# Slot table from one-hots of 64, logits on four column groups, and half of the first low weight halves back on VectorE

## The chip, the cores and the metric

The kernel runs on one core of a Trainium2 chip. The time is that of one execution on the device in microseconds (us); a kernel is run several times, and the median counts.

## The reference: windowed attention, then a two-level mixture of experts

```python
# q, k, v: (8, 8, 576, 64) f32
scores = q @ k.transpose(0, 1, 3, 2) / 8
# heads 0 to 3: 0 <= i - j < 32; heads 4 to 7: 0 <= i - j < 128 and (i - j) % 4 == 0
scores = np.where(masks[None], scores, -1e9)
attn = softmax(scores) @ v
x = attn.transpose(0, 2, 1, 3).reshape(4608, 512)
# 4 groups of 4 experts, one group and one expert in it per token
g_idx = argmax(x @ w_group); g_w = softmax(x @ w_group)[g_idx]
e_idx = argmax(x @ w_expert[g_idx]); e_w = softmax(x @ w_expert[g_idx])[e_idx]
h = maximum(x @ w1[g_idx, e_idx], 0)        # 512 -> 1024
out = g_w * e_w * (h @ w2[g_idx, e_idx])    # 1024 -> 512
```

Each of the 4608 tokens goes to one of 16 experts. A matmul of f32 quality is made from two f16 halves of each operand, high and low, and three products of them.

## The kernel before: 36 attention steps with the routing woven in, then 16 experts

**Attention.** The batches go in pairs (`bp`, 0 to 3), and each pair in nine steps of 64 positions, so there are 36 steps `s` and three more to empty the pipeline. In step `s` TensorE (PE) computes `scores(s)`, `av(s - 2)` (probabilities times values), `transpose_p(s - 1)` and `transpose_x(s - 3)`; VectorE (DVE) takes the maxima `mx` (L281) and differences `d` (L283) of the scores, and with `den` (L362, L364) normalises the result to `x` (L369); ScalarE (ACT) does the exponentials and copies. `o`, the PSUM tile of `av`, exists once, so that `av` of one step waits for `x` of the step before. GpSimd (POOL) makes shifted copies of `v` (`shift_v`, L130 to L137, tile `vs`, two in turn, one for three steps), and for the first group of a pair clears the part of `kb` that carries keys over (L118).

**Routing.** After the nine steps of a pair, `turned_logits` (L416, then L417 on ACT) computes the gate logits of its 1152 tokens, nine tiles of 128 (`TPB`), and the generator `route` does the rest in pieces. `slot()` is called between DVE's attention instructions and runs pieces as long as a credit lasts, which grows by `RATE[bp]` a call. A piece that yields 2 closes a gate: what follows, PE work, is put behind the next step's `av`. `route` transposes the logits (L424, `lg_ps`), finds group and expert (L433 to L456, the one-hot `E`), counts ranks by matmuls (L462 to L467, `rk_ps`), and turns each token's slot, an expert's base plus a rank, into a table of tokens by slot: a one-hot `ohl` of the slot's low 7 bits (L506) times `mv`, a one-hot of its high part times the token's number (L495, L502), summed over tiles by matmuls (L517, `tb_ps`), added into `tab` (L538 to L543). `own` is a PSUM tile that holds small operands of DVE.

**Hand-over.** For the two experts that have most tokens after two and three pairs, weights are loaded early (`prefetch`, `load_weights`): eight chunks of 128x1024, the high half `h` on ACT (L640), the low half `l` on DVE (L637), or with `aside`, for the first expert, on GpSimd (L634, L635). Their first 128 and 256 tokens are computed beside the last steps and the last routing; there the order is the string `TAIL`, a letter for a piece: `r` of the last routing, `a` and `b` of the first and second expert, `w` a chunk of weights, `T` the end of the routing's PSUM tiles. After it the experts follow one another (L726 first layer, L734 low half `hl` of its result, L819 and L837 second layer).

PE and DVE have their orders from the code (`manual_schedule`, L926), SP and ACT as well from the start (L140); GpSimd's is left to the scheduler until the experts.

## Time and profile before

| what | value |
|---|---|
| median of 3 runs | 571.64 us (571.36 to 571.8) |
| profiled execution, own time | 573.72 us |
| its span | 572.0 us |
| mean granted TensorE clock | 0.995 of full speed |
| busy share: PE, PEld, DVE, ACT, POOL | 94%, 68%, 66%, 56%, 38% |
| DMA | 134.32 MB, mean 235 GB/s |

PEld is the loading of weights into TensorE, which overlaps its matmuls. A share is an average over the attention steps (to some 150 us), the hand-over and the experts, which have different limits; idle time of an engine costs something only where another waits for it.

### The profile page before, as it was taken

How to read it: one execution, taken by the hardware profiler on the slowest of the kernel's cores; microseconds unless marked ns; L12 is line 12 of the kernel's file. 1: busy time of each engine (PE TensorE's matmuls, PEld its weight loads, DVE VectorE, ACT ScalarE, POOL GpSimd, SP SyncE). 2: the span in 40 equal slices, each digit the busy share in tenths (PEclk: the TensorE clock that was granted, in tenths of full speed). 3: DMA queues.
4: the chain of work that ended last, by engine and by line, in shares of the span. 5: the costliest groups of instructions: out<-in, count | busy, mean ns of one | idle time of the engine just before them, and what ended most of it. 6: DMA issues, size and time to landing. Idle time of an engine off the chain costs nothing. (4 is left out here: it accounts for less than half of the span.)

```text
span 572.0 us, 16623 instructions
## 1 busy us (share of the span) xinstructions
PE 539.1 (94%) x6652; PEld 390.1 (68%) x6652; DVE 376.4 (66%) x853; ACT 318.7 (56%) x563; POOL 218.2 (38%) x204
## 2 busy tenths in 40 slices
PE   4999999997797999999999999999999999999975
PEld 2788778786675676557666667576675775797873
DVE  8675886968778337464859597755757757766730
ACT  6464554565654236464656465565666665774631
POOL 6795554649920423402140523225153231121202
PEclk9999999999999999999999999999999999999989
DMA  7988878799672716968697786969879899879811
GB/s 275 390 282 262 311 271 269 257 312 283 187 254 62 235 41 173 296 156 243 191 280 199 250 216 210 295 187 311 211 241 293 239 285 321 223 275 296 221 60 30
DMA packets 79266, 134.32 MB, mean 235 GB/s; under 512 B 42988, under 2 KB 52630, under 8 KB 79186
## 3 DMA queue, kind: packets, MB, share of 16 engines
q1 hardware_dynamic: 72258, 113.65, 65.7%
q0 software_dynamic: 6784, 19.51, 10.4%
q8 instruction: 54, 0.88, 0.6%
q14 instruction: 26, 0.21, 0.1%
q10 hardware_dynamic: 144, 0.07, 0.1%
HBM read 106.16 MB, written 19.29 MB: 219 GB/s over the span
## 5 line engine op out<-in xcount | busy, mean ns | idle before, releaser
L790 POOL DMA_INDIRECT out<-yr,sent x31 | 35.3, 1139 | 218.9 <-ACT yr L789 205.9
L734 DVE SCALAR_TENSOR_TENSOR hl<-a,hh 128x256 f16<-128x256 f32 (+13 forms) x144 | 60.8, 423 | 83.2 <-ACT hh L733 83.1
L726 PE MATMUL a<-xs,wb1h 128*128 128x256 f16 (+7 forms) x576 | 97.7, 275 | 2.1 <-DVE hl L734 2.1
L726 PE MATMUL a<-xs,wa 128*128 128x304 f16 (+7 forms) x864 | 98.3, 275 | 0.3 <-SPq L1134 0.3
L733 ACT ACTIVATE hh<-a 128x256 f16<-128x256 f32 (+13 forms) x144 | 55.9, 388 | 65.8 <-PE a L726 64.3
L726 PEld LDWEIGHTS <-wa 128*128 128x128 f16 x864 | 80.7, 99 | 17.0 <-SPq L1134 0.5
L637 DVE SCALAR_TENSOR_TENSOR wa<-w,wa 128x1024 f16<-128x1024 f32 x56 | 67.7, 1217 | 27.6 <-ACT wa L640 27.6
L819 PEld LDWEIGHTS <-hh 128*128 128x128 f16 x480 | 46.9, 98 | 54.8 <-issue 1.2
L640 ACT ACTIVATE wa<-w 128x1024 f16<-128x1024 f32 x64 | 67.2, 1055 | 21.0 <-DMA w<-wpack 16.3
L726 PE MATMUL a<-xs,wb1l 128*128 128x256 f16 (+7 forms) x288 | 78.3, 275 | 0.0
L819 PE MATMUL y<-wa,hh 128*128 128x512 f16 x240 | 73.9, 379 | 0.0
L726 PEld LDWEIGHTS <-wb1h 128*128 128x128 f16 x576 | 55.0, 98 | 14.5 <-issue 2.6
L665 POOL DMA_INDIRECT xr<-xd,sent x41 | 41.6, 1014 | 38.0 <-DVE key L590 14.5
L637 DVE SCALAR_TENSOR_TENSOR wb2l<-w,wb2h 128x1024 f16<-128x1024 f32 x32 | 38.6, 1220 | 20.3 <-ACT wb2h L640 20.3
L313 PE MATMUL o<-vs,pt 128*32 128x130 f32 x576 | 40.6, 274 | 8.8 <-DVE x L369 3.7
L302 ACT COPY pt<-t 128x512 f32<-128x512 f32 x36 | 21.1, 586 | 49.1 <-PE t L301 48.5
L789 ACT ACTIVATE yr<-y,cs 128x512 f32<-128x512 f32 (+3 forms) x31 | 21.3, 686 | 44.2 <-PE y L819 32.3
L819 PE MATMUL y<-wb2h,hh 128*128 128x512 f16 x120 | 45.6, 380 | 0.0
L819 PE MATMUL y<-wa,hl 128*128 128x512 f16 x120 | 45.5, 379 | 0.0
L819 PE MATMUL y<-wb2h,hl 128*128 128x512 f16 x120 | 45.5, 379 | 0.0
L819 PE MATMUL y<-wb2l,hh 128*128 128x512 f16 x120 | 45.5, 379 | 0.0
L640 ACT ACTIVATE wb2h<-w 128x1024 f16<-128x1024 f32 x32 | 33.2, 1052 | 16.3 <-DMA w<-wpack 16.0
(202 smaller groups left out, 1069.2 us busy)
## 6 DMA issues: line engine op xcount, KB each, us to landing
w<-wpack SPq DMA_DIRECT2D x128, 512.0 KB
kb<-k SPq DMA_DIRECT2D x24, 384.0 KB
vt<-v SPq DMA_DIRECT2D x14, 390.0 KB
qb<-q SPq DMA_DIRECT2D x7, 768.0 KB
xd<-x SPq DMA_DIRECT2D x24, 192.0 KB
wa<-v SPq DMA_DIRECT2D x6, 390.0 KB
wa<-q SPq DMA_DIRECT2D x3, 768.0 KB
xd<-x SPq DMA_DIRECT2D x32, 48.0 KB
```

The lines of the kernel that those rows point to most:

```text
L302: nc.scalar.copy(pt[n % NPT], t)
L313: nc.tensor.matmul(o[32 * j : 32 * j + 32, c // 2, at : at + 130], pt[n % NPT][:, c, 32 * j : 32 * j + 32], t[:, :, jl, bb * 4 + c, :], st ...
L637: nc.vector.scalar_tensor_tensor(l, w32, SW, h, ALU.mult, ALU.subtract)
L640: nc.scalar.mul(parts(i)[0], w32s[i], SW)
L665: nc.gpsimd.indirect_dma_start(out=xr[0:n], out_offset=None, in_=xd[0:known, :], in_offset=bass.IndirectOffsetOnAxis(ap=ent[0:n, t : t + 1 ...
L726: nc.tensor.matmul(a[:, 0:cap], ww[:, c * FF + f * P : c * FF + f * P + P], xx[:, c, 0:cap], start=(i == 0), stop=(i == len(mm) - 1),)
L733: nc.scalar.activation(hh[:, f, 0:cap], a[:, 0:cap], AF.Relu)
L734: nc.vector.scalar_tensor_tensor(hl[:, f, 0:cap], a[:, 0:cap], 0.0, hh[:, f, 0:cap], ALU.max, ALU.subtract)
L789: nc.scalar.activation(yr[0:n, :], yp[0:n, :], AF.Copy, scale=cs[0:n, t : t + 1])
L790: ins = nc.gpsimd.indirect_dma_start(out=out, out_offset=bass.IndirectOffsetOnAxis(ap=ent[0:n, t : t + 1], axis=0), in_=yr[0:n, :], in_off ...
L819: nc.tensor.matmul(yp, h[:, f, t * P : t * P + n], ww[:, f * DM : f * DM + DM], start=(i == 0), stop=(i == len(mm) - 1),)
```

## The change: smaller one-hots, GpSimd's products, a fourth column group

A slot's low part now has 6 bits, so `ohl` has 64 columns, in one DVE instruction. An expert has 8192 slots of room (`REG`), so that the bits above say only which of the first eight blocks of 64 a token is in: DVE makes `okm`, a one-hot of eight per token. GpSimd multiplies it by the token's number and then by the expert's one-hot `E`, once for the even and once for the odd blocks, into `mv`. The table's matmuls write 64 partitions each, two for each tile. The logits run on four column groups of PE (32 columns each) instead of three: four tiles at a time, and for the ninth each group adds one quarter of the features, summed when `id4` turns them. Of the first expert's eight low halves, four (the second, fourth, sixth and eighth) go to DVE. GpSimd's order is taken from the code, too; `RATE` and `TAIL` have new values.

```diff
-RATE = (0.23, 0.3, 0.45)
+RATE = (0.2, 0.25, 0.4)
-TAIL = "ararrrarrawrawwrawbwarrrrrrrbrrwbrrwbrrrrwbrrrrTwbbb"
+TAIL = "ararrrarrawrrawrwarrrwbwarrrbrwrbrrwbrrrwbrrrTwbbb"
-REG = NTOK + P
+REG = 8192
...
+    id4 = cp.tile([P, 32], F32, name="id4")
+    nc.vector.tensor_reduce(id4, id32.rearrange("p (q m) -> p m q", q=4), axis=AX.X, op=ALU.add)
...
-        lt_ps = psR.tile([96, 3, P], F32, name="lt_ps", tag="r")
+        lt_ps = psR.tile([P, 3, P], F32, name="lt_ps", tag="r")
         for i in range(3):
             chains = []
-            for j in range(3):
-                a0 = (3 * i + j) * P
+            for j in range(4):
+                a0 = min(4 * i + j, TPB - 1) * P
                 cuts = [a0] + [S] * (a0 < S < a0 + P) + [a0 + P]
-                chains.append([(c, j, a, b, a0) for a, b in zip(cuts, cuts[1:]) for c in range(4)])
+                own_c = range(4) if i < 2 else (j,)
+                chains.append([(c, j, a, b, a0) for a, b in zip(cuts, cuts[1:]) for c in own_c])
...
-                    nc.tensor.matmul(ov, wg[:, c], mv, start=(c == 0), stop=(c == 3))
+                    nc.tensor.matmul(ov, wg[:, c], mv, start=(c == 0 or i == 2), stop=(c == 3 or i == 2))
...
-        for i in range(3):
-            nc.tensor.transpose(
-                lg_ps[:, 3 * i : 3 * i + 3].rearrange("p t n -> p (t n)"), lt[:, i], id32[0:96, 0:96]
-            )
+        for i in range(2):
+            nc.tensor.transpose(lg_ps[:, 4 * i : 4 * i + 4].rearrange("p t n -> p (t n)"), lt[:, i], id32)
+        nc.tensor.matmul(lg_ps[:, TPB - 1], lt[:, 2], id4, start=True, stop=True)
...
-        mv = T("mv", [TPB, NE * NK4], F16)
+        okm = T("okm", [TPB, 2 * NK4])
         nc.vector.tensor_tensor(
-            mv,
-            high_v.unsqueeze(1).broadcast_to([P, TPB, NE * NK4]),
-            hl[:, 1].unsqueeze(2).broadcast_to([P, TPB, NE * NK4]),
+            okm,
+            low_v[:, 0 : 2 * NK4].unsqueeze(1).broadcast_to([P, TPB, 2 * NK4]),
+            hl[:, 1].unsqueeze(2).broadcast_to([P, TPB, 2 * NK4]),
             ALU.is_equal,
         )
-        yield 0.75
-        nc.vector.tensor_tensor(mv, mv, mine_v.unsqueeze(2).broadcast_to([P, TPB, NE * NK4]), ALU.mult)
-        yield 0.75
-        ohl = T("ohl", [TPB, P], F16)
-        for t0 in range(0, TPB, 3):
-            nc.vector.tensor_tensor(
-                ohl[:, t0 : t0 + 3],
-                low_v.unsqueeze(1).broadcast_to([P, 3, P]),
-                hl[:, 0, t0 : t0 + 3].unsqueeze(2).broadcast_to([P, 3, P]),
-                ALU.is_equal,
+        mv = T("mv", [2, TPB, NE, NK4], F16)
+        nc.gpsimd.tensor_tensor(okm, okm, mine1.unsqueeze(2).broadcast_to([P, TPB, 2 * NK4]), ALU.mult)
+        okv = okm.rearrange("p t (k h) -> p h t k", h=2)
+        for h in range(2):
+            nc.gpsimd.tensor_tensor(
+                mv[:, h],
+                Ef[:, 0:TPB].unsqueeze(3).broadcast_to([P, TPB, NE, NK4]),
+                okv[:, h].unsqueeze(2).broadcast_to([P, TPB, NE, NK4]),
+                ALU.mult,
             )
-            if t0 < TPB - 3:
-                yield 0.55
+        yield 0.2
+        ohl = T("ohl", [TPB, 64], F16)
+        nc.vector.tensor_tensor(
+            ohl,
+            low_v.unsqueeze(1).broadcast_to([P, TPB, 64]),
+            hl[:, 0].unsqueeze(2).broadcast_to([P, TPB, 64]),
+            ALU.is_equal,
+        )
+        yield 2
         yield 2
...
         for t in range(TPB):
-            nc.tensor.matmul(tb_ps, ohl[:, t], mv[:, t], start=(t == 0), stop=(t == TPB - 1))
+            for h in range(2):
+                nc.tensor.matmul(
+                    tb_ps[64 * h : 64 * h + 64],
+                    ohl[:, t],
+                    mv[:, h, t].rearrange("p e k -> p (e k)"),
+                    start=(t == 0),
+                    stop=(t == TPB - 1),
+                )
...
-            todo.extend(load_weights(ev[r], wsets[r], r == 0))
+            todo.extend(load_weights(ev[r], wsets[r], lambda i: r == 0 and i % 2 == 0))
...
-    man.enter_context(tc.manual_schedule(engines={ET.PE, ET.DVE}))
+    man.enter_context(tc.manual_schedule(engines={ET.PE, ET.DVE, ET.Pool}))
```

The order in which instructions stand shows what this moves; the lines of the changed kernel are numbered differently there. First GpSimd near the start: the shifts of `v` into the two tiles `vs`, and the memset of `kb` (L118). Before:

```order
L130 TENSOR_SCALAR vs_112<-vt_110 64x2x1040
L133 TENSOR_SCALAR vs_112<-vt_110 64x2x520
L137 TENSOR_SCALAR vs_113<-vt_110 64x2x520
L118 MEMSET kb_115 128x2x256
L130 TENSOR_SCALAR vs_113<-vt_111 64x2x1040
L133 TENSOR_SCALAR vs_113<-vt_111 64x2x520
L130 TENSOR_SCALAR vs_113<-vt_111 64x2x520
```

And now, where the same memset stands:

```order
L130 TENSOR_SCALAR vs_112<-wa_92 64x2x520
L133 TENSOR_SCALAR vs_112<-wa_92 64x2x520
L130 TENSOR_SCALAR vs_113<-vt_110 64x2x1040
L135 MEMSET vs_113 64x2x520
L133 TENSOR_SCALAR vs_113<-vt_110 64x2x520
L118 MEMSET kb_115 128x2x256
L130 TENSOR_SCALAR vs_113<-vt_110 64x2x520
```

The memset stood ahead of the second tile's first shift (from `vt_111`); now it stands behind the shifts of two more groups (from `vt_111` and from `wa_92`) and most of the fourth's (`vt_110` again).

Second DVE, where the third pair's routing begins (`pm`, `oh`, `E` are pieces of the argmax, `mx` and `d` of attention). Before:

```order
L448 TENSOR_REDUCE pm_2529<-own 128x45
L369 TENSOR_TENSOR x<-o,den 128x512
L451 TENSOR_TENSOR oh_2536<-own,pm_2529 128x180
L456 TENSOR_TENSOR E_206<-oh_2536 128x144
L281 TENSOR_REDUCE mx<-s 128x8
L283 TENSOR_TENSOR d<-s,mx 128x4x2x64
L362 TENSOR_SCALAR den<-o 128x8
L477 TENSOR_TENSOR rks<-rk_ps,E_206 128x144
```

And now (L642 is the low half of a weight chunk, L637 before):

```order
L440 TENSOR_REDUCE pm_2547<-own 128x45
L361 TENSOR_TENSOR x<-o,den 128x512
L443 TENSOR_TENSOR oh_2554<-own,pm_2547 128x180
L642 SCALAR_TENSOR_TENSOR wa_91<-w_2190,wa_91 128x1024
L273 TENSOR_REDUCE mx<-s 128x8
L448 TENSOR_TENSOR E_208<-oh_2554 128x144
L275 TENSOR_TENSOR d<-s,mx 128x4x2x64
L354 TENSOR_SCALAR den<-o 128x8
L356 RECIPROCAL den<-den 128x8
```

A low half stands ahead of `E`, and the ranks' first instruction (L477 before, L469 now) comes a whole step later.

Third DVE in the hand-over, where the last pair is routed beside the second expert's weights (`wb1l` is one of its low halves). Before:

```order
L451 TENSOR_TENSOR oh_3176<-own,pm_3158 128x180
L734 SCALAR_TENSOR_TENSOR hl<-a,hh 128x128
L637 SCALAR_TENSOR_TENSOR wb1l<-w_3016,wb1h 128x1024
L637 SCALAR_TENSOR_TENSOR wb1l<-w_3018,wb1h 128x1024
L456 TENSOR_TENSOR E_207<-oh_3176 128x144
L637 SCALAR_TENSOR_TENSOR wb1l<-w_3020,wb1h 128x1024
```

And now:

```order
L443 TENSOR_TENSOR oh_3200<-own,pm_3182 128x180
L448 TENSOR_TENSOR E_209<-oh_3200 128x144
L739 SCALAR_TENSOR_TENSOR hl<-a,hh 128x128
L642 SCALAR_TENSOR_TENSOR wb1l<-w_3034,wb1h 128x1024
L642 SCALAR_TENSOR_TENSOR wb1l<-w_3036,wb1h 128x1024
L469 TENSOR_TENSOR rks<-rk_ps,E_209 128x144
L471 COPY base_159<-rk_ps 128x16
```

`E` moved ahead of the two low halves. On PE the ranks, which need it, moved from behind the first expert's second layer to ahead of it.

## Rows read from the trace of the kernel before

**Rows 1.** The page's busy tenths of PE in 40 equal slices of the span.

```profile
PE   4999999997797999999999999999999999999975
```

**Rows 2.** Busy time by stretches of 20 us: the stretch, its length, then for each engine the busy us and the number of instructions, the granted clock as a share of full speed, the DMA share and GB/s. Engines in order: PE, PEld, DVE, ACT, POOL.

```profile
160.00:180.00 20.00, 17.45 (x167) 13.24 (x165) 17.96 (x41) 12.51 (x21) 1.16 (x2) 1.00 0.58 196
...
220.00:240.00 20.00, 20.00 (x148) 11.72 (x147) 13.73 (x24) 12.05 (x19) 4.41 (x5) 1.00 0.99 280
```

**Rows 3.** The timeline of PE: start, length of the row, line, operation, tiles. L254 begins a step, L271 are its scores, L313 its `av`, L462 the ranks, L517 the table. In brackets the idle time before, and what ended it.

```profile
38.21 1.08 PE L271 MATMUL s<-kb,qb 128*32 128x128 f32 x32
...
57.74 0.38 PE L254 MATMUL s<-masks,idb 128*128 128x512 bf16 x1
...
64.86 0.44 PE L462 MATMUL rk_ps<-base,id 128*128 128x160 f32 x2
...
65.56 0.38 PE L254 MATMUL s<-masks,idb 128*128 128x512 bf16 x1
...
79.78 0.42 PE L517 MATMUL tb_ps<-mv,ohl 128*128 128x64 f16 x9
80.04 0.38 PE L254 MATMUL s<-masks,idb 128*128 128x512 bf16 x1
...
83.18 0.38 PE L254 MATMUL s<-masks,idb 128*128 128x512 bf16 x1
...
92.76 0.38 PE L254 MATMUL s<-masks,idb 128*128 128x512 bf16 x1
...
118.36 0.38 PE L254 MATMUL s<-masks,idb 128*128 128x512 bf16 x1
...
128.53 0.38 PE L254 MATMUL s<-masks,idb 128*128 128x512 bf16 x1
...
136.15 0.27 PE L313 MATMUL o<-vs,pt 128*32 128x130 f32 x1 [1.04 <-DVE top L564]
...
140.53 0.27 PE L313 MATMUL o<-vs,pt 128*32 128x130 f32 x1 [1.04 <-DVE x L369]
...
146.60 0.42 PE L517 MATMUL tb_ps<-mv,ohl 128*128 128x64 f16 x9
```

**Rows 4.** The timeline of POOL, same columns: shifts of `v` (L130, L133, L137), memsets of `kb` (L118) and `vs` (L135).

```profile
17.48 1.05 POOL L137 TENSOR_SCALAR vs<-vt 64x1040 f32<-64x1040 f32 x1
19.74 0.53 POOL L118 MEMSET kb<- 128x512 f32 x1 [1.21 <-PE s L271]
22.35 1.93 POOL L130 TENSOR_SCALAR vs<-vt 64x2080 f32<-64x2080 f32 x1 [2.08 <-DMA vt<-v]
24.36 1.05 POOL L133 TENSOR_SCALAR vs<-vt 64x1040 f32<-64x1040 f32 x1
...
28.65 0.96 POOL L135 MEMSET vs<- 64x1040 f32 x1
...
35.10 1.93 POOL L130 TENSOR_SCALAR vs<-vt 64x2080 f32<-64x2080 f32 x1
```

**Rows 5.** The timeline of PE: the first pair's logits (80 records, two for each f32 matmul), and the transposes of the logits.

```profile
49.41 2.93 PE L416 MATMUL lt_ps<-xT,wg 128*32 128x128 f32 x80
...
57.49 0.41 PE L424 MATMUL lg_ps<-id,lt 96*128 96x96 f32 x3
```

**Rows 6.** Groups of DVE instructions of one shape between 50 and 190 us: line, operation, tiles, out and in (partitions x elements, type), count, then busy us in total, mean ns of one, idle us before them.

```profile
L506 DVE TENSOR_TENSOR ohl<-own,hl 128x384 f16<-128x384 f32 x12 | 6.4, 536 | 0.0
L637 DVE SCALAR_TENSOR_TENSOR wb2l<-w,wb2h 128x1024 f16<-128x1024 f32 x4 | 4.9, 1214 | 0.0
...
L495 DVE TENSOR_TENSOR mv<-own,hl 128x576 f16<-128x576 f32 x4 | 3.0, 753 | 0.0
L502 DVE TENSOR_TENSOR mv<-mv,own 128x576 f16<-128x576 f16 x4 | 3.0, 743 | 0.0
...
L538 DVE TENSOR_SCALAR own<-tb_ps 128x64 f32<-128x64 f32 x4 | 0.9, 218 | 0.0
```

**Rows 7.** The timelines of POOL (two low-half pieces of the first expert) and of DVE beside them, and one more L646 of DVE with POOL idle.

```profile
148.97 2.14 POOL L635 TENSOR_TENSOR wa<-w,wa 128x1024 f16<-128x1024 f32 x1
151.08 1.05 POOL L634 TENSOR_SCALAR w<-w 128x1024 f32<-128x1024 f32 x1
...
149.64 1.52 DVE L646 TENSOR_TENSOR sel<-tab,top 128x32 f32<-128x32 f32 x1
...
151.41 0.74 DVE L653 CAST ente<-twoe 128x2 int32<-128x2 f32 x1
...
182.93 0.23 DVE L646 TENSOR_TENSOR sel<-tab,top 128x48 f32<-128x48 f32 x1
```

**Rows 8.** The timelines of PE and DVE in the hand-over.

```profile
163.19 0.38 PE L819 MATMUL y<-wa,hh 128*128 128x512 f16 x1
...
175.95 0.26 PE L517 MATMUL tb_ps<-mv,ohl 128*128 128x64 f16 x3 [1.50 <-DVE ohl L506]
...
180.50 0.38 PE L726 MATMUL a<-xs,wb1h 128*128 128x256 f16 x2 [1.16 <-DVE hl L734]
...
182.73 0.38 PE L726 MATMUL a<-xs,wb1h 128*128 128x256 f16 x2 [0.76 <-DVE hl L734]
...
163.22 0.33 DVE L451 TENSOR_TENSOR oh<-own,pm 128x180 f32<-128x180 f32 x1
...
166.44 0.30 DVE L456 TENSOR_TENSOR E<-oh 128x144 bf16<-128x144 f32 x1
```

More of the change, by code (lines that the diff above doesn't have):

```diff
@@ L173, in moe_attention_kernel @@
     own = psV.tile([P, 512], F32, name="own")
-    low_v, high_v, pri, mine_v = own[:, 0:P], own[:, P : P + NE * NK4], own[:, 192:196], own[:, 196 : 196 + TPB]
+    low_v, pri = own[:, 0:64], own[:, 192:196]
     oh_v = own[:, 208 : 208 + 20 * TPB].rearrange("p (n e) -> p n e", e=4)
@@ L209, in moe_attention_kernel @@
     slots = cp.tile([P, NCHK], F32, name="slots")
-    high = cp.tile([P, NE, NK4], F32, name="high")
-    nc.gpsimd.iota(
-        high,
-        pattern=[[REG // P, NE], [1, NK4]],
-        base=0,
-        channel_multiplier=0,
-        allow_small_or_imprecise_dtypes=True,
-    )
-    nc.vector.tensor_copy(low_v, low)
-    nc.vector.tensor_copy(high_v, high.rearrange("p e k -> p (e k)"))
-    nc.vector.tensor_copy(mine_v, mine1)
+    nc.vector.tensor_copy(low_v, low[:, 0:64])
     tab = cp.tile([P, NE, NK4], F32, name="tab")
@@ L403, in turned_logits @@
     def turned_logits(bp):
-        lt = sm.tile([96, 3, P], F32, name="lt")
-        lt_ps = psR.tile([96, 3, P], F32, name="lt_ps", tag="r")
+        lt = sm.tile([P, 3, P], F32, name="lt")
+        lt_ps = psR.tile([P, 3, P], F32, name="lt_ps", tag="r")
         for i in range(3):
             chains = []
-            for j in range(3):
-                a0 = (3 * i + j) * P
+            for j in range(4):
+                a0 = min(4 * i + j, TPB - 1) * P
                 cuts = [a0] + [S] * (a0 < S < a0 + P) + [a0 + P]
-                chains.append([(c, j, a, b, a0) for a, b in zip(cuts, cuts[1:]) for c in range(4)])
+                own_c = range(4) if i < 2 else (j,)
+                chains.append([(c, j, a, b, a0) for a, b in zip(cuts, cuts[1:]) for c in own_c])
             for k in range(max(map(len, chains))):
@@ L422, in route @@
         lg_ps = psR.tile([P, TPB, 32], F32, name="lg_ps", tag="r")
-        for i in range(3):
-            nc.tensor.transpose(
-                lg_ps[:, 3 * i : 3 * i + 3].rearrange("p t n -> p (t n)"), lt[:, i], id32[0:96, 0:96]
-            )
+        for i in range(2):
+            nc.tensor.transpose(lg_ps[:, 4 * i : 4 * i + 4].rearrange("p t n -> p (t n)"), lt[:, i], id32)
+        nc.tensor.matmul(lg_ps[:, TPB - 1], lt[:, 2], id4, start=True, stop=True)
         T = lambda nm, shape, dt=F32: sm.tile([P] + shape, dt, name=nm)
@@ L487, in route @@
         nc.vector.tensor_copy(sl_v[:, 2], slots[:, mine])
-        nc.vector.tensor_single_scalar(sl_v[:, 1], sl_v[:, 2], 7, ALU.arith_shift_right)
+        nc.vector.tensor_scalar(sl_v[:, 1], sl_v[:, 2], 6, P - 1, ALU.arith_shift_right, ALU.bitwise_and)
         yield 0.35
-        nc.vector.tensor_single_scalar(sl_v[:, 0], sl_v[:, 2], P - 1, ALU.bitwise_and)
+        nc.vector.tensor_single_scalar(sl_v[:, 0], sl_v[:, 2], 63, ALU.bitwise_and)
         hl = T("hl", [2, TPB], F16)
@@ L608, in order, with load_weights @@
         nc.vector.tensor_copy(ordi[:, NEARLY:NE], ordf[:, NEARLY:NE])
-    def load_weights(ev, w, aside=False):
+    def load_weights(ev, w, aside=lambda i: False):
         src = wpack[bass.ds(ev * P, P), :]
@@ L632, in chunk @@
                 h, l = parts(i - 1)
-                if aside:
+                if aside(i - 1):
                     nc.gpsimd.tensor_scalar(w32, w32, SW, 1.0, ALU.mult, ALU.mult)
```

## The prediction

> **What bounds the kernel now.** I read the page first: its row of TensorE (PE) slices shows nines almost everywhere and sevens near a quarter of the span [rows 1]. The busy time by stretches then says where PE can gain: 17.45 of 20 us are busy at 160 to 180, 20.00 at 220 to 240, with the granted clock at full speed in both [rows 2]. Whatever delays PE after its expert matmuls have become continuous costs its own length, and before that only PE's own work, and waits of PE, can move the end. So I followed PE by its timeline through the attention steps and the hand-over to the experts (up to about 186 us), and looked at the other engines where PE waits.
>
> One attention step without routing takes 3.14 us of PE: from 80.04 to 83.18 [rows 3]. Seven such steps are 21.98. The seven from 57.74 to 83.18, in which the first batch pair is routed, take 25.44; PE's own routing matmuls in them are 0.70 for the ranks (64.86 to 65.56) and 0.26 for the table (79.78 to 80.04), so PE waits 2.5 us. The second pair's seven, from 92.76 to 118.36, hold 25.60 - 21.98 - 0.96 = 2.66 us of waits; the third pair's four, from 128.53 to 146.60, 18.07 - 12.56 - 0.70 = 4.8 [rows 3]. The waits of the third end about when VectorE (DVE) has written `x`, or another of its pieces, with 1.04 us each at 136.15 and 140.53: DVE is full there, and its work counts one to one.
>
> The profiled execution took 573.72 us around a span of 572.0. The runs' median is 571.64, 2.08 lower, so I sum the changes of the profiled span and add the sum to 571.64. Three runs lie within 0.44 us; I call anything within 0.2% (1.14 us) no change.
>
> **The change part by part.**
>
> *GpSimd in program order: +1.6.* Before, GpSimd ran the memset of the carried keys (L118, `kb`) at 19.74, while it had nothing better to do: it then waited until 22.35 for `v` to land [rows 4]. Now the memset stands behind the third group's shifts. In the row before, the third group's large shift starts at 35.10, with GpSimd busy without a break since 22.35. Now it has as many pieces ahead of it (L137 twice and no L135, instead of once each, 1.05 against 0.96 us), so it starts at 35.2. It takes 1.93, the memset L135 0.96, one shift of 1.05, and then L118 0.53; with three gaps of 0.08 (22.35 + 1.93 to 24.36) that ends at 39.9 [rows 4]. PE wants those keys at 38.21 [rows 3], so it waits about 1.6 us, in steps that hold no other wait to absorb it. Bounds: 0, if the queue ahead shortens, and 1.9. The later two memsets come in stretches in which GpSimd is not behind, and I cost them at nothing; its slack covers them.
>
> *Logits on four column groups: -2.2.* Today 40 matmuls per pair take 2.93 us [rows 5]. Three chains run side by side, of 128 columns a round: four rounds for the first three tiles, five for the second three (the tile cut at 576 has eight halves on one group, and its last four run nearly alone), four for the third: 13 rounds of 128 columns, 0.225 us a round. With four chains it is 4, then 5.5 (the same eight halves), then one for the ninth tile: 10.5 rounds, 2.37 us. Four pairs give -2.2. If a fourth chain gains nothing, 0; if time falls as 3 to 4, -0.73 a pair. The Trainium skill (TensorEngine Tiling (Array Packing), Performance Considerations) promises up to four times for weights of 32 columns. By it alone the step from three groups to four would be 3/4, -2.9 in all. I keep -2.2, because the ordered rounds already account for the 2.93 of the row.
>
> *Turning the logits back, and the table: +0.7.* Three passes of 96 columns take 0.25 us (57.49 to 57.74) [rows 3, 5]. Two passes of 128 are 256 of the same 288 columns; the f32 matmul by `id4` is new, nearest the two-pass rank start at 64.86. I take +0.15 a pair (0 to 0.3). The table's nine matmuls become eighteen of half width on two groups; nine take 0.26 [rows 3], so between 0 and +0.26 a pair, near 0 because the logits' groups run side by side: +0.1 in all.
>
> *Table work off DVE, pairs one and two: -1.3.* Gone are 753 + 743 + 3 x 536 ns = 3.10 us; new are `okm`, like a 64-element row of 218, and one `ohl` of 576 elements, like 753: 0.97 [rows 6]. So 2.13 us less DVE work a pair, against waits of 2.5 and 2.66. Ends 0 and -2.13 a pair. I take -0.65: the removed instructions stand in about four of seven steps, and the first waits (behind `lg_ps` and `rk_ps`) do not depend on them.
>
> *Third pair: +1.5.* It loses the same 2.13, but three of the low halves that GpSimd computed (the second, fourth and sixth) come back to DVE, 1.21 each [rows 6]: +3.64. DVE being full, +1.5. The order shows the second right behind `oh`, with the ranks a step later. There is also a conflict. DVE's L646, with two SBUF inputs, took 1.52 us against 0.23 elsewhere and ended when GpSimd's L635 did; L653 took 0.74 and ended with L634 [rows 7]. Today that costs some 1.9 us. The Trainium skill (SBUF — State Buffer, Who interferes with whom) says that a DVE instruction with two SBUF inputs and a GpSimd instruction that reads SBUF exclude each other, whoever starts first; those rows agree. Every returned low half has two SBUF inputs, and GpSimd gets three new multiplications a pair. I let the same 1.9 stay. Ends: -0.4 if it vanishes, +3.6 with one more hold of L635's 2.14.
>
> *Hand-over: -0.4.* PE's table waits 1.50 for `ohl` at 175.95, and later 1.16 and 0.76 for `hl` [rows 8], with DVE full. DVE has 2.13 less to do; the eighth low half falls into its idle time before. But the ranks now stand ahead of the first expert's second layer: PE gets there at 163.19, while `E`, today at 166.44, can follow `oh` at about 163.55 and take 0.30, so PE waits about 0.7 [rows 8]. And the table needs `mv` from GpSimd: 2 x 576 elements at L635's 2.14 us for 1,024 are 2.4 us behind `okm`; it waits about 2.5 rather than 1.5 + 0.2. So 0.7 + 0.8 - 1.9 = -0.4, between -2.1 and +1.5.
>
> Sum: 1.6 - 2.2 + 0.7 - 1.3 + 1.5 - 0.4 = -0.1, so 571.5.
>
> **The rivals.** *DVE was the whole bound.* If pairs one and two give back all 2.13 each, the sum becomes -3.1: 568.5. It decides once they give 2.4 instead of 1.3. For it: waits that end at `x`. Against: part of each wait stands in steps that lose nothing. Chance 0.25. *The memset comes in time.* Then the 1.6 goes: 569.9. Against it speaks the unbroken row on GpSimd; 0.10. *DVE and GpSimd hold each other more* (slower). Two of the three returned low halves held 1.3 us, as L646 was, add 2.6: 574.1; one such hold decides. For it: both engines get such work in the same steps. Against: where DVE comes first, GpSimd waits, and nobody waits for it. This is the mechanism of the SBUF page's rule. 0.23. *The fourth group gains nothing*: +2.1, 573.7; 0.04. My forecast, that gains and losses cancel, has 0.38.
>
> **How the numbers follow.** No change 0.38; faster 0.25 + 0.10 = 0.35; slower 0.23 + 0.04 = 0.27. The forecast's own range is 570.5 to 572.6. For eight in ten I go to 568.9 and 573.9, which leave out the ends of the first and third rivals.
>
> **What would show each step.** A wait of PE for GpSimd's `kb` near 38 to 40 us, and the next step that much later; logits of 2.37 us; waits of about 1.9 us in each of the first two pairs; DVE's returned low halves near 1.2 us, or longer with GpSimd busy beside them; PE waiting for `E` behind the last logits and for `mv` at the last table. The prediction is wrong if the first is missing, if a low half takes 2 us or more, or if PE's continuous run starts over 1.14 us earlier or later.

## The result: 0.9% slower, with a spread from chip to chip

The kernel before took 571.59 us and the changed kernel 578.18 us (medians of 18 runs each). A ratio leaves out the executions that took over 1.5% longer than the fastest of their kernel; it is 1.0093, with a 95% interval of 1.0064 to 1.0122. The forecast was no change, 571.5 us in a range of 568.9 to 573.9. The five groups of experiments below ran on the chips numbered 13, 0, 2, 14 and 0, and chips differ: the kernel before took 573.6, 580.8, 582.2, 574.0 and 582.3 us in them. So each ratio is to the kernel before on the same chip; the changed kernel, run again on chip 2, gave 1.0022 (0.999 to 1.0055).

The profiled execution of the changed kernel took 577.76 us around a span of 576.0, against 573.72 and 572.0. Its page, the busy tenths in 40 equal slices of PE, of the granted clock and of the DMA engines:

```profile
span 576.0 us, 16700 instructions
...
PE   4899998988687899999999999999999999999985
...
PEclk9999999999698999999999999999999999999999
DMA  8988888896684252959596969688797898898741
```

PE's row answers [rows 1]: its weakest slice but for the first and the last is now the eleventh (144 to 158 us), with a 6, and the clock row has a 6 in the same place. Where the time went is read from four points on PE: the scores of step 13, where the first logits have just ended; step 32, where the third pair's routing begins; the last logits; and the first expert's second `y`, from which PE runs on without long waits. These are starts in PE's timelines, in us, and below them the difference of the two kernels over each stretch:

```
                 step 13   step 32   last logits   second y    end
before             53.21    128.53        157.15     185.35   571.98
changed            54.65    130.04        164.41     194.50   576.02
later by            1.44    + 0.07        + 5.75     + 1.89   - 5.11
```

The four stretches of the working in the prediction come to +1.05 (the memset, less the first logits), -1.9, +1.5 and -0.8 (the hand-over with the last logits and their turning). The first two pairs gave nothing instead of 1.9 us, and the third pair with the first expert's start lost 5.75 instead of 1.5. The last column is a second surprise: of 9.15 us that PE starts its expert run late, the end shows 4. Near the end PE waits for ScalarE, which waits for the last experts' weights, and it waited more in the kernel before: 3.99 us in waits over 0.25 us, against 1.78. Behind that the granted clock was 0.73 of full speed from 550 to 555 us, where the changed kernel has 1.00. First the kernel before, then the changed one (the stretch, its length, busy us and instructions of each engine, granted clock, DMA share, GB/s):

```profile
540.00:550.00 10.00, 6.78 (x124) 6.37 (x122) 3.95 (x4) 4.54 (x8) 1.52 (x2) 0.97 0.55 170
```
```profile
540.00:550.00 10.00, 10.00 (x112) 7.17 (x110) 8.56 (x14) 6.26 (x10) 2.43 (x2) 1.00 0.96 224
550.00:555.00 5.00, 3.22 (x60) 2.98 (x58) 2.14 (x2) 2.68 (x4) 0.25 (x1) 1.00 0.42 153
```

**The third pair.** The same view of the changed kernel where it lost most:

```profile
140.00:144.00 4.00, 3.30 (x81) 2.54 (x75) 3.86 (x11) 1.75 (x4) 3.94 (x3) 1.00 0.01 2
144.00:148.00 4.00, 0.98 (x34) 0.74 (x29) 3.81 (x14) 1.40 (x4) 3.81 (x3) 1.00 0.19 25
148.00:152.00 4.00, 3.41 (x36) 2.62 (x27) 1.06 (x3) 2.18 (x4) 3.84 (x5) 0.54 0.96 306
152.00:156.00 4.00, 3.23 (x39) 2.47 (x38) 3.49 (x7) 2.20 (x4) 4.00 (x3) 0.50 0.79 244
```

The DMA engines stand still from 140 to 144 us (share 0.01), PE is busy for 0.98 of the next 4 us, and then the granted clock falls to the lower of its two levels (1.2 GHz, 0.50), where PE's 6.6 busy us in the next eight are worth 3.5 at full speed, an estimate by these shares. Two engines stand behind this. The first is GpSimd (POOL); its timeline, with its idle time before an instruction in brackets:

```profile
130.45 1.16 POOL L670 DMA_INDIRECT xe<-xd,ente  x1 [12.08 <-DVE den L354]
137.89 1.92 POOL L130 TENSOR_SCALAR vs<-vt 64x2080 f32<-64x2080 f32 x1 [6.27 <-DMA vt<-v]
139.89 1.05 POOL L137 TENSOR_SCALAR vs<-vt 64x1040 f32<-64x1040 f32 x1
140.91 1.05 POOL L133 TENSOR_SCALAR vs<-vt 64x1040 f32<-64x1040 f32 x1
141.93 2.00 POOL L639 TENSOR_SCALAR w<-w 128x1024 f32<-128x1024 f32 x1
```

The first low half (L639) starts at 141.93; in the kernel before the same piece (L634) starts at 121.91. In program order it stands behind a gather that waits 12.08 us, until the stores into `xd`, which it reads, have landed (the last, L540, at 129.51), and behind shifts that wait 6.27 us for `v`. The weights keep their buffer meanwhile: in SyncE's queue a load waits 7.5 us, until 146.18, for the low half's second piece (L640) to end. ScalarE (ACT), whose `pt` copies stand behind the next high half, waits for that load; and the DMAs behind it in SyncE's queue, stores of `x` among them, land so late that VectorE's (DVE's) next `x` waits 3.10 us for them:

```profile
149.82 1.06 ACT L645 ACTIVATE wa<-w 128x1024 f16<-128x1024 f32 x1 [3.52 <-DMA w<-wpack]
...
152.45 0.69 DVE L361 TENSOR_TENSOR x<-o,den 128x512 f32<-128x512 f32 x1 [3.10 <-DMA w<-wpack]
```

The second is VectorE, whose `x` ends the long wait of PE. It has no idle time between the `x` at 140.26 and the next at 146.63, and what stands between them is the third pair's routing and a returned low half. It is held there, too: one of its returned low halves (L642) takes 1.21 us, the next 1.89 beside GpSimd's shifts and L639, which itself takes 2.00 instead of 1.05. PE waits 3.02 us for that `x`, and most of this wait is not the late weights': with GpSimd's order left free (the first run below) it is still 2.35 us, the low half then taking 1.21:

```profile
132.50 1.21 DVE L642 SCALAR_TENSOR_TENSOR wa<-w,wa 128x1024 f16<-128x1024 f32 x1
...
141.15 1.89 DVE L642 SCALAR_TENSOR_TENSOR wa<-w,wa 128x1024 f16<-128x1024 f32 x1
```
```profile
147.46 0.38 PE L305 MATMUL o<-vs,pt 128*32 128x130 f32 x2 [3.02 <-DVE x L361]
...
181.00 0.19 PE L516 MATMUL tb_ps<-mv,ohl 128*64 128x64 f16 x1 [1.13 <-POOL mv L497]
183.12 0.64 PE L516 MATMUL tb_ps<-mv,ohl 128*64 128x64 f16 x17 [1.93 <-POOL mv L497]
```

The last two rows are the hand-over: the table waits 3.06 us in all for `mv`, where 1.50 stood before [rows 8]. GpSimd multiplies `okm` only behind a scatter, and the two products, DVE's low halves beside them, take 3.30 us:

```profile
178.31 1.03 POOL L795 DMA_INDIRECT out<-yr,ente  x1 [11.68 <-ACT yr L794]
179.35 0.34 POOL L494 TENSOR_TENSOR okm<-okm,mine 128x72 f32<-128x72 f32 x1
179.77 3.30 POOL L497 TENSOR_TENSOR mv<-E,okm 128x576 f16<-128x576 bf16 x2
```

**The first two pairs.** The keys' memset comes 0.64 us late, and the logits answer [rows 5] with 2.19 us instead of 2.93. But PE has a kind of idle time in which it waits for nothing that the profile shows ("issue"), in the middle of a row of like matmuls: 1.10 us in the kernel before ahead of 170 us, 5.36 now, such as 1.52 us in the scores behind the second pair's logits. The third pair's logits have 1.01 us of it inside, and take 3.43 us.

```profile
39.40 1.08 PE L263 MATMUL s<-kb,qb 128*32 128x128 f32 x32 [0.64 <-POOL kb L118]
...
51.60 2.19 PE L409 MATMUL lt_ps<-xT,wg 128*32 128x128 f32 x80
...
90.94 0.97 PE L263 MATMUL s<-kb,qb 128*32 128x128 f32 x28 [1.52 <-issue]
```

### The profile page after: what moved, and what is told of

Same layout as the page of the kernel before. It is cut to its first block, busy times and chain, and to the rows that moved or that the text cites. A ratio compares the mean times of both kernels' runs of the same rounds, so it can differ in the third digit from the quotient of the medians.

```text
span 576.0 us, 16700 instructions
## 1 busy us (share of the span) xinstructions
PE 538.6 (94%) x6692; PEld 389.3 (68%) x6692; DVE 374.1 (65%) x844; ACT 319.4 (55%) x563; POOL 218.5 (38%) x207
## 5 line engine op out<-in xcount | busy, mean ns | idle before, releaser
L731 PE MATMUL a<-xs,wa 128*128 128x304 f16 (+7 forms) x864 | 97.0, 273 | 0.0
L642 DVE SCALAR_TENSOR_TENSOR wa<-w,wa 128x1024 f16<-128x1024 f32 x60 | 73.7, 1235 | 25.8 <-ACT wa L645 25.8
L642 DVE SCALAR_TENSOR_TENSOR wb2l<-w,wb2h 128x1024 f16<-128x1024 f32 x32 | 39.5, 1243 | 19.4 <-ACT wb2h L645 18.6
L273 DVE TENSOR_REDUCE mx<-s 128x8 f32<-128x512 f32 x36 | 24.7, 687 | 26.3 <-PE s L263 26.3
```

The lines of the kernel that those rows point to most:

```text
L273: nc.vector.tensor_reduce(mx, s, axis=AX.X, op=ALU.max)
L642: nc.vector.scalar_tensor_tensor(l, w32, SW, h, ALU.mult, ALU.subtract)
L731: nc.tensor.matmul(a[:, 0:cap], ww[:, c * FF + f * P : c * FF + f * P + P], xx[:, c, 0:cap], start=(i == 0), stop=(i == len(mm) - 1),)
```

## The experiments

Given for each run: the ratio to the kernel before and its interval; then, in us of its profile, which is of one execution, from step 32 to 35, from there to the last logits, and PE's "issue" idle time in pieces over 0.25 us between 20 and 170 us. The kernel before has 13.96, 14.66 and 1.10; the changed kernel 13.01, 21.36 and 5.36.

**Order and halves.** Theory A: GpSimd's program order is the cause. Theory B: the halves on VectorE are. The first run undoes the order:

```
-    man.enter_context(tc.manual_schedule(engines={ET.PE, ET.DVE, ET.Pool}))
+    man.enter_context(tc.manual_schedule(engines={ET.PE, ET.DVE}))
```

> The changed kernel, but GpSimd's order is left to the scheduler again, as in the kernel before; everything else stands. In the changed kernel the first low half on GpSimd (L639) starts at 141.93 us, behind a gather (L670 at 130.45) and three shifts that wait for v (137.89); in the kernel before it starts at 121.91. ScalarE then waits 3.52 us for a weight load at 149.82. Theory A, GpSimd's program order is the cause: the first low half starts near 122 to 125 us again, ScalarE's wait for the load is gone, PE's continuous expert run starts at or before the 185.35 us of the kernel before, and the time is 567 to 570.5 us (the logits' -0.75 us a pair and the shorter waits of the first two pairs remain). Theory B, the low halves back on VectorE and what they do beside GpSimd's are the cause: only the 0.64 us wait for the keys goes, and the time is 575 to 578 us.

Measured: 1.0158 (1.011 to 1.0207); 15.15, 16.48, 2.89. The first low half starts at 121.53 again and the last stretch loses 4.9 us against the changed kernel, as A expects, but the time is above what either gave. The profiled execution was the fastest of six, and its granted clock is 1.00 from 140 to 160 us. Over the six the time follows the mean granted clock: 575.19 us at 0.997, 579.00 at 0.989, 581.57 to 585.90 at 0.981 to 0.983. The kernel before took 573.62 us there, with a median of 0.998.

The second keeps the order and puts all low halves back on GpSimd (`lambda i: r == 0`).

> The changed kernel, but all eight low halves of the first expert stay on GpSimd, as in the kernel before; GpSimd keeps its program order. Theory B (the halves on VectorE are the cause): 568 to 571 us, and VectorE's 1.89 us low half at 141.15 is gone. Theory A (GpSimd's order is the cause): the queue behind the gather and the shifts gets four low halves longer, 3.2 us each, the weight loads come later still, and the time is 578 to 584 us.

Measured: 1.0327 (1.028 to 1.0375); 12.62, 32.87, 1.69. The third gives GpSimd its program order in the kernel before.

> The kernel before with one edit: GpSimd keeps its program order too. All eight low halves are on GpSimd there. Theory A: the first low half starts after 135 us rather than at 121.91, ScalarE waits for a weight load, and the time is 577 to 585 us. Theory B: only the wait for the keys' memset comes, 0.6 to 1.6 us, 572 to 573.5 us.

Measured: 1.0238 (1.0187 to 1.0288), 14.0 us; 13.96, 28.51, 1.53. ScalarE waits twice for a weight load, with the DMA engines at a share of 0.00:

```profile
148.44 1.06 ACT L640 ACTIVATE wa<-w 128x1024 f16<-128x1024 f32 x1 [8.97 <-DMA w<-wpack]
158.74 1.06 ACT L640 ACTIVATE wa<-w 128x1024 f16<-128x1024 f32 x1 [7.44 <-DMA w<-wpack]
```

The fourth undoes both.

> The changed kernel with both undone: GpSimd's order left to the scheduler and all eight low halves on GpSimd. What remains is the logits on four column groups, the small table and its products on GpSimd. Both theories give 567.5 to 570.5 us. If Theory A holds and the halves on VectorE cost nothing, it equals the run with the free order alone within 1 us; if the halves help, it is slower than that run.

Measured: 1.0118 (1.0064 to 1.0172); 13.57, 18.80, 4.80. Here, too, the profiled execution was the fastest of six, 575.15 us at a mean clock of 0.997, and the slowest took 584.65 at 0.981. So the order by itself costs 13 to 14 us, with or without the rest of the change, and the halves on VectorE give it back: it is one bargain, and what is left of the two together cannot be told from nothing here (1.0118 without them, 1.0093 and 1.0022 with them, on three chips). Neither theory explains the loss alone; with both undone it is still there, 1.5 us above the median of the kernel before where the clock stayed up, and more where it was lower; no profile of these two forms shows such an execution. What remains is the logits, the table and the new places of the last routing.

**Logits, table and places, apart.** The logits alone, in the kernel before (`turned_logits`, the turning back and `id4`):

> The kernel before with the logits on four column groups alone (and the two transposes and the matmul by id4 that turn them back). Theory D, the logits' gain is kept: 2.12 instead of 2.87 us in each of four pairs, +0.11 for turning back, so 2.5 us less: 569 to 570.5 us. Theory C, PE runs ahead of its instructions: 80 matmuls and 80 weight loads in 2.12 us use up what is loaded, and the idle time inside a row of like matmuls that waits for nothing ('issue') behind or inside the logits grows by about what they gained (0.46 to 1.94 us in the changed kernel and in the two of its forms with the low halves or the order undone, 0 to 0.74 in the kernel before): 571 to 574 us.

Measured: 0.9924 (0.9886 to 0.9963); 13.97, 14.73, 6.44. Faster by 0.8%, though its profile has the idle time that theory C expects. Its timeline of PE, the stretch of the wait, and the DMA queues between 127.5 and 127.7 us, where a block of instructions begins to load, 1.7 us after the logits' end and with the DMA engines full. PE had stopped at 127.42, before that load began, and goes on 1.4 us after it has landed, so the load is no proof of the theory:

```profile
123.75 2.21 PE L419 MATMUL lt_ps<-xT,wg 128*32 128x128 f32 x80
130.12 0.80 PE L273 MATMUL s<-kb,qb 128*32 128x128 f32 x9 [2.70 <-issue]
```
```profile
128.00:130.00 2.00, 0.00 (x0) 0.00 (x0) 0.00 (x0) 1.99 (x4) 2.00 (x2) 0.92 1.09 353
```
```profile
q8 instruction: 1, 0.02, 32.8%
```

The table alone, with the last routing in its old places:

> The kernel before with the small table alone: one-hots of 64, the products on GpSimd, and the rates of the routing that go with it; logits on three groups, all low halves on GpSimd, its order left to the scheduler, and the last routing in its old places (two empty steps fill those that the table no longer needs). If the products on GpSimd are the cause of the loss (PE waits 1.13 and 1.93 us for mv at the last table, and in the third pair three more instructions stand between the low halves): 575 to 579 us. If they are not: 568.5 to 572 us, since VectorE has 2.13 us less a pair.

Measured: 0.9975 (0.9946 to 1.0005); 12.39, 18.97, 1.47. Three us gained up to step 35, 4.3 lost behind it. Both together in the old places:

> Logits on four groups and the small table with its rates; all low halves on GpSimd, its order left to the scheduler, as in the run with both undone (579.26), but with the last routing in its old places (ranks behind the first expert's second layer). If the new places are the cause (PE waits 0.27 us for E and is turned to the ranks 0.5 us early; the table stands where mv is 3 us away): 571 to 574 us. If they are not: 577 to 581 us, as with the new places.

Measured: 0.9997 (0.9969 to 1.0025); 12.39, 19.13, 4.14. And with both undone, but the last pair's products on VectorE:

```
-        nc.gpsimd.tensor_tensor(okm, okm, mine1...)
+        eng = nc.vector if bp == NBP - 1 else nc.gpsimd
+        eng.tensor_tensor(okm, okm, mine1...)      # and the two of mv
```

> The run with both undone (579.26), but the three products of the last pair's table on VectorE instead of GpSimd; the other pairs' stay there. If PE's 3.06 us of waits for mv at the last table, and the clock that falls behind them, are the cause: 1.5 to 4 us less than that run, 575 to 578 us, and no wait for GpSimd at the table. If not: within 1 us of it.

Measured: 0.9983 (0.995 to 1.0017); 13.56, 17.75, 4.62. The stretch behind step 35 is long in every run so far in which GpSimd makes the third pair's products. In the kernel before GpSimd was as full there as VectorE (fifth column of busy times):

```profile
136.00:140.00 4.00, 3.34 (x73) 2.58 (x73) 3.76 (x17) 2.08 (x5) 3.83 (x3) 1.00 0.95 311
140.00:144.00 4.00, 3.35 (x73) 2.59 (x73) 4.00 (x10) 2.38 (x7) 3.84 (x4) 1.00 0.86 272
```

What the table alone shows there is a cast of two numbers (0.17 us elsewhere) that takes 1.93 beside one subtraction on GpSimd, and PE's wait for the `x` behind it:

```profile
153.51 1.93 DVE L659 CAST ente<-twoe 128x2 int32<-128x2 f32 x1
```
```profile
153.30 2.12 POOL L641 TENSOR_TENSOR wa<-w,wa 128x1024 f16<-128x1024 f32 x1
```
```profile
156.41 0.87 PE L381 MATMUL tx<-id,x 128*128 128x128 f32 x4 [3.23 <-DVE x L359]
```

**The products on VectorE.** First the changed kernel again, as the yardstick of this chip:

> The changed kernel as it is, on the same chip as the three runs beside it, as their yardstick. The kernel before took 571.6, 573.6 and 580.8 us on the three chips so far. If the loss belongs to the program and not to one chip, the ratio to the kernel before is 1.006 to 1.012 again, and the profile shows idle time inside rows of like matmuls of 3 to 6 us ahead of 170 us and a wait of ScalarE for a weight load near 150 us.

Measured: 1.0022 (0.999 to 1.0055); 13.01, 19.39, 3.00. PE starts its second `y` at 194.98, as late as in the first profile. The loss of time is smaller here; there is no profile of the kernel before on this chip that could say why.

> The changed kernel with GpSimd's order left to the scheduler, all low halves on GpSimd, and the products of the third and fourth pair's tables on VectorE (those of the first two stay on GpSimd); the last routing in its new places. Theory E, GpSimd is full from 128 to 157 us (3.42 to 3.92 of every 4 us in the kernel before) and every product put there delays low halves, weight loads and in the end PE (from the last scores to the last logits 14.7 us without the products on GpSimd, 18 to 19 with them): that stretch falls to 14.5 to 16 us and the time is 3 to 5 us below the run with both undone, a ratio of 0.995 to 1.005. Theory F, the new places of the last routing are the cause: the ratio stays near that run's 1.012.

Measured: 0.9976 (0.9938 to 1.0015); 18.08, 13.67, 5.58.

> The small table alone, with the last routing in its old places and the logits on three groups, and the products of the third and fourth pair on VectorE. Theory E: 14.5 to 16 us from the last scores to the last logits instead of 18.97, and a ratio of 0.990 to 0.995, as the first two pairs keep their gain of 1.3 us and the third gives nothing back. If the products on GpSimd cost nothing, the ratio is that of the small table alone, 0.9975.

Measured: 0.9957 (0.9921 to 0.9992); 17.74, 14.76, 3.37.

> As the run before it, with the logits on four groups too: the form that should beat both kernels. If both gains add up (0.9924 for the logits alone, about 0.993 for this table): 0.985 to 0.990. If what PE gains in the logits it loses again waiting for its instructions (2.7 to 6.4 us of such idle time ahead of 170 us where the logits run on four groups, 1.1 to 1.5 where they run on three): 0.990 to 0.997, no better than the run before it.

Measured: 0.9937 (0.9898 to 0.9976); 16.03, 14.89, 3.13. In all three theory E gets its stretch, 13.7 to 14.9 us, but 2.1 to 4.1 us turn up ahead of it, from step 32 to 35. These forms also have the third pair's `RATE` back at 0.45 and credits of their own for the products, and what the 2.1 to 4.1 us owe to that is not separated. But the products are held there. In the run of the table alone, VectorE and, beside its first product, GpSimd:

```profile
139.06 2.46 DVE L499 TENSOR_TENSOR mv<-E,okm 128x576 f16<-128x576 bf16 x1
...
142.64 1.42 DVE L499 TENSOR_TENSOR mv<-E,okm 128x576 f16<-128x576 bf16 x1
```
```profile
138.99 1.93 POOL L130 TENSOR_SCALAR vs<-vt 64x2080 f32<-64x2080 f32 x1
```

**An operand out of SBUF.** Theory H: VectorE's instructions with all operands in SBUF are held while GpSimd works in SBUF. The old table had an operand in PSUM in each of its steps (`high_v`, `mine_v`, `low_v` are views of `own`); the new products have none.

```
+        if on_dve:                                  # third and fourth pair
+            okm = own[:, 64 : 64 + 2 * NK4 * TPB].rearrange("p (t k) -> p t k", k=2 * NK4)
...
-        select(ente[r], top[:, r], 0, NET[r], sm.tile([P, 4], F32, name="twoe"))
+        select(ente[r], top[:, r], 0, NET[r], own[:, 184:188])
```

> Logits on four groups and the small table with late products on VectorE, the old places (the last run before this), with two tiles moved to PSUM: okm of the third and fourth pair, and the two numbers twoe from which the cast makes the rows to gather. Theory H, VectorE's instructions with all operands in SBUF are held while GpSimd works in SBUF: the first product takes 0.75 us instead of 2.44, the cast 0.2 instead of 0.76, PE's waits of 3.09 and 1.10 us for x fall to about 1.0 and 0.3, from the scores of step 32 to the last logits it is 28 us instead of 30.9, and the ratio falls by 0.3 to 0.5%, to 0.988 to 0.991. If VectorE is late for another reason: the ratio stays at 0.994.

Measured: 0.9936 (0.9902 to 0.997). The profiled execution was the longest of twelve, so the rows are from the last run of this section, which has the same tiles: there the products take 0.75 and 0.74 us, the cast 0.16, and the two stretches 28.5 us instead of 30.9. The ratio did not fall below that of the run before it, 0.9937 with nearly the same interval.

```profile
138.45 0.75 DVE L504 TENSOR_TENSOR mv<-E,own 128x576 f16<-128x576 bf16 x1
140.32 0.74 DVE L504 TENSOR_TENSOR mv<-E,own 128x576 f16<-128x576 bf16 x1
...
153.71 0.16 DVE L668 CAST ente<-own 128x2 int32<-128x2 f32 x1
```

> The small table alone with its products on GpSimd and the old places, with twoe in PSUM. There the cast took 1.93 us at 153.51, beside one of GpSimd's subtractions, and PE then waited 3.23 us. Theory H: the cast takes about 0.2 us, PE's wait falls to 1.3 us, from the last scores to the last logits it is 16.5 to 17.5 us instead of 18.97, and the ratio falls from 0.9975 to about 0.995. If the cast was only waiting its turn in a row that is late anyway: no change.

Measured: 0.9983 (0.9947 to 1.002); 12.45, 16.27, 4.88. The cast takes 0.16 us, PE's wait falls from 3.23 to 1.47, the stretch is just below the 16.5 to 17.5 us of H, 2.7 us shorter; no difference in the time can be told.

> The logits on four groups alone, with twoe in PSUM. The logits alone gave 0.9924; the kernel before holds the cast by 0.6 us at 151.41. Theory H: up to 0.6 us less, 0.991 to 0.9925, and the cast at 0.2 us.

Measured: 0.9999 (0.9965 to 1.0034); 13.97, 14.20, 4.13. The stretch is 0.5 us shorter, but the 0.9924 of the logits alone does not return on this chip: what they are worth lies between nothing and 0.8%.

The last of this group slows the logits' pace and keeps their instructions (`for chain in chains` instead of the rounds across chains):

> The logits on four column groups, but the four chains one after the other instead of side by side: the same 80 matmuls and 80 weight loads, the same places, only slower. Theory C (PE runs ahead of its instructions when it takes 160 in 2.1 us): idle time inside rows of like matmuls ahead of 170 us is 0 to 1.5 us, as in the kernel before, instead of the 6.4 us of the side-by-side form; the logits themselves take 1 to 4 us longer a pair, and the time is above that of the kernel before, by 2 to 12 us. If the idle time belongs to the new instructions and not to their pace, it stays at 3 us or more.

Measured: 1.0081 (1.0051 to 1.011), 4.4 us; 13.97, 14.72, 1.62. The logits take 4.75 us, 2.5 more, and none of the idle time that is left stands behind them (1.4 of the 1.6 us is at 27.7 us):

```profile
51.17 4.75 PE L419 MATMUL lt_ps<-xT,wg 128*32 128x128 f32 x80
```

**What separates the change from its repaired form.** The changed kernel with the tiles in PSUM and the late products on VectorE; and that with all low halves on GpSimd and its order free, so that only the new places of the last routing differ from `d1_psum`:

> The changed kernel (GpSimd in program order, half of the low halves on VectorE, new places of the last routing) with the two tiles of the earlier run in PSUM and the products of the third and fourth table on VectorE. What is left between it and that run (0.9936) is order, halves and places. If order and halves cost what they gave in the profile (first low half on GpSimd 20 us late, ScalarE waiting 3.52 us for a weight load): 1.000 to 1.008, with that wait again, and 18 us or more from the last scores to the last logits. If the products and the cast were the whole loss: 0.992 to 0.997.

Measured: 0.9969 (0.9934 to 1.0005); 14.36, 19.39, 3.57. The stretch is as long as expected, but not for the reason given: ScalarE waits only 0.87 us for a load, and PE waits 2.09, 0.89 and 2.02 us for VectorE, whose low halves are held:

```profile
138.78 1.96 DVE L652 SCALAR_TENSOR_TENSOR wa<-w,wa 128x1024 f16<-128x1024 f32 x1
...
150.67 1.79 DVE L652 SCALAR_TENSOR_TENSOR wa<-w,wa 128x1024 f16<-128x1024 f32 x1
```

> The same two tiles in PSUM and late products on VectorE, all low halves on GpSimd and its order left to the scheduler, but the last routing in the new places. Against the run with the old places (0.9936) only the places differ. If the new places cost the 0.3 to 0.8 us that PE turns to the ranks too early and waits at the last table (6.6 instead of 6.0 us from the last logits to the first expert's second layer): 0.994 to 0.996. If they are worth nothing either way: 0.9925 to 0.9945.

Measured: 0.9881 (0.9826 to 0.9935), 575.8 us against 582.3; 14.36, 14.16, 3.87. The first low half is back at 120.81 us. The new places cost nothing that shows, and on this one chip order and halves together cost 0.9% by the ratios, whose intervals just touch (medians 579.7 against 575.8 us). This is the form with the lowest ratio, from six runs: logits on four groups, the small table, products on GpSimd for the first two pairs and on VectorE with `okm` in PSUM for the others, low halves on GpSimd in an order that the scheduler chooses.

## Why the prediction was wrong, step by step

- **"What bounds the kernel."** Right that PE's waits ahead of 186 us decide, and that what delays its expert run then counts; wrong that it counts in full. Of 9.15 us, 4.04 were left at the end in one profile. The working had no term for PE's waits near 545 us [rows 1: the last slices] and the clock behind them; the 2.2 us of waits and an estimated 1.4 us at the share of 0.73 that the kernel before had more there make up some 3.6 of the 5.1 us; the rest is not accounted for. By the prediction's own signs the start of the expert run, 9.15 us late, is what proved it wrong.
- **GpSimd in program order, +1.6, with the sentence "its slack covers them".** This step failed. The memset itself cost 0.64 us, inside the bounds (the terms there add up to 39.91 less 38.21, 1.7 rather than 1.6). But the working followed only the memsets; it did not ask what else the order moves past GpSimd's waits. The first low half moved by 20 us, and two pairs of runs show 13 to 14 us for the order alone; order and halves together cost 3.9 us in the last pair. Every instruction behind a gather or a load that waits had to be listed, and then who waits for the buffer that it holds: the weight loads, and behind them ScalarE and the stores of `x`.
- **Logits, -2.2.** The size was too small: 2.19 instead of 2.93 us, -0.74 a pair where nothing breaks the row. The Trainium skill (TensorEngine Tiling (Array Packing), Performance Considerations) gives a factor of four for 32 columns; the estimate from it, a quarter less than on three groups, -2.9 in all, was the better guide, and the trace agrees with it. But the gain does not arrive whole: on three groups the five profiles without the new logits have 1.1 to 4.9 us of "issue" idle time, mean 2.5; the fourteen with them side by side 1.7 to 6.4, mean 4.2. By the means, 1.8 of the 3.0 us that the four logits could gain would be lost to it, but the ranges overlap. With the pace slowed one profile has 1.6, which three groups have too. So neither the pace nor the late loading of instructions is shown to be the cause; both are argued.
- **Turning back and table, +0.7.** Inside its bounds: 0.36 instead of 0.25, and 0.41 instead of 0.26 us a pair, +1.0 in all.
- **First two pairs, -1.3.** About right. From 59.00 to 83.67 and from 94.12 to 119.33 PE takes 24.67 and 25.21 us instead of 25.44 and 25.60 [rows 3], although the table takes 0.15 more in each: -1.5.
- **Third pair, +1.5, bounds -0.4 to +3.6.** This step failed in size: +5.75. It took VectorE as the one full engine and let "the same 1.9 stay". GpSimd was full too, 3.8 of every 4 us, and with its three new products the stretch grew to 18.97 us from 14.66 for the table alone; 2.7 of these 4.3 us are gone with one cast out of SBUF (16.27). The low half that VectorE got back, beside the routing, made PE wait 3.02 us for `x`, against 1.04 at most before. Held instructions grew, as the third rival said: 1.89 us for a low half, 2.00 for GpSimd's scaling. And no term priced what followed that wait: at the lower clock PE's 3.41, 3.23 and 4.00 busy us in 148 to 160 us lost an estimated 4.5 us by the granted shares 0.54, 0.50 and 0.68 of those stretches.
- **Hand-over, -0.4, bounds -2.1 to +1.5.** Outside its bounds: the stretch grew by 1.89 us although the last logits gained 0.74. `mv` came 3.06 us late rather than 2.5, since GpSimd reached `okm` only behind a scatter, and its products took 3.30 instead of 2.4 us; behind these waits the granted shares were 0.80 and 0.77 from 180 to 188 us. The wait for `E` was 0.27, not 0.7.
- **The rivals.** "DVE and GpSimd hold each other more", slower, 574.1, had the side and a part of the mechanism; its size counted holds alone, without the loads and the clock. The Trainium skill's rule behind it (SBUF — State Buffer, Who interferes with whom) is borne out by 2.46 us for a product with two SBUF inputs against 0.75 with one in PSUM. The same section of the Trainium skill says that casts too can take the shared ports; the cast of 1.93 us, 0.16 from PSUM, agrees. The working had counted a cast's 0.74 us in its 1.9, but gave two SBUF inputs as the only condition.

What stays open: why the granted clock was lower in most executions of the first group's forms, where the profiled ones of the two with the order left free kept it; and why the changed kernel loses 0.9% on one chip and, if anything, 0.2% on another.

## What to carry to other kernels

Before an engine is put into program order, list for each instruction what stands ahead of it that waits for a load, a gather or another engine, and then who waits for the buffer that it frees; a memset on a queue is the least of it. When work moves from a full engine to another, read the other's busy time in the same stretch, not over the span. Where VectorE and GpSimd work side by side, keep one operand of VectorE's instructions in PSUM: two tiles moved took a product from 2.46 to 0.75 us and a cast from 1.93 to 0.16 us. The time itself did not show it: 0.9937 and 0.9936, 0.9975 and 0.9983, 0.9924 and 0.9999 without and with it, each pair on two chips. And before a profile is held against a median, see where its execution stands among the others: two profiles here were of the fastest of six, 7 and 4 us below the medians.

## What the runs showed of the hardware that was not expected

PE can stand still with nothing to wait for that the profile shows: with the logits alone it did so for 2.70 us, 1.5 us behind 160 records (matmuls and weight loads) issued in 2.2 us, with the DMA engines at a share of 1.01 to 1.09. It does so in profiles with the logits on three groups as well (2.2 us inside them in one), so pace is not its only condition, and its cause stays open. And one wait of PE can cost more than its length: behind 0.98 busy us of 4, in a wait of 3.02 us, the granted share was 0.54 and 0.50 for eight us. With GpSimd's order free, 1.73 busy us of 4 in the same place were followed by 1.00.
